# Four small moves in a fused recurrence and expert kernel: a store, six copies, two loads, and the first unit of the newer form

## The chip, the cores and the metric

The kernel runs on one core of one Trainium2 chip. The metric is the device time of one execution in microseconds; 962.84 us is the median of the three runs before the change.

## What is computed

A gated linear recurrence per batch and head feeds four dense experts whose outputs are mixed by normalised probabilities. Shapes: batch 4, 8 heads, 768 steps, head size 48; so x has 3072 rows of 384, and each expert goes 384 -> 1024 -> 384.

```python
for t in range(S):                       # per batch and head
    state = alpha[t][:, None] * state + outer(k[t], v[t])
    y[t] = q[t] @ state
x = y rearranged to (batch * step, head * 48)
p = domain_probs / (domain_probs.sum(-1) + 1e-9)
out = sum over e of p[:, e] * (relu(x @ w1[e]) @ w2[e])
```

## The kernel before, in words

**Units and groups.** The recurrence is cut into 24 units, each one block of 128 steps of one batch with all 8 heads (`units`, counted from 0). They are put into groups: group 0 has units 0 and 1, groups 1 to 5 have four units each (2 to 5, 6 to 9, and so on), group 6 the last two. The experts run over a group at a time (`tasks`): for each expert, `up` makes eight tiles of the hidden layer (L993, or L997 for the very first expert), and `down` multiplies them with w2 (L1081). In group 0 the first expert uses raw weights; after that every weight is split into two parts (ScalarE L261, VectorE L263) and stored for later groups by GpSimd (`kept<-w`, L264); later groups load the parts with SyncE (`w<-kept`, L234). In `up` from group 1 on, ScalarE makes the upper part of the hidden tile (L1001) and VectorE the lower one (L1033). VectorE's instruction is also the last reader of the PSUM tile `one`; `one` and the sums `ops` of `down` share four PSUM buffers, so the fifth tile of a row waits for the first L1033.

**The recurrence within a unit.** A unit's scores are built in seven levels of decay. Each level multiplies half of q and half of k by a factor (VectorE), makes the next level's factors (GpSimd, L788 or L557), copies q into block form (ScalarE, `qb`), and copies the half of the keys that stays the same. TensorE then makes score products, which VectorE takes under masks into `near`, and finally the unit's result and the update of the state.

There are two forms of a unit. `attention` (units 2 to 7 and, for the most part, 1) has four places on TensorE: scores of levels 0 to 3, then the last levels (L861 and L805), then a turn of the keys through TensorE (L295), then the result (L900, L481). `in_order` (from `in_fours`, unit 8, on) treats groups of four steps on GpSimd (L515, L518, L519; VectorE sums them in L529), so its levels 0 and 1 need no scores, and it turns the keys with VectorE (L639) and a round trip through DRAM: SyncE stores them as `over` (L648) and reads them back as `AT` (L655). All its TensorE work stands in one place, the step called the burst: the result of the unit before (L676, L695) and its own scores (L602, L612). Unit 0 is done by `first_unit` with an order of its own.

**What sets the order.** Each unit is a generator; `deal` gives each of its steps a planned time from a table of fractions, and `advance` runs the steps whose time has come while `up` and `down` are written out. Every engine executes its own instructions in the order written. For units 6 to 9 the ends are planned at 101.1, 132.8, 164.5 and 196.2, unit 5's at 63.4 and unit 4's at 50.7 (planned time, in which group 1's first expert begins at 69.4). An old-form unit begins at most two slots before its end; unit 6 begins at 50.7. A new-form unit has its burst at the end of the unit before and its head in the slot before that: the first one by `HEAD_FIRST` (first step at 0.06 of that slot), the second by `HEAD_SECOND`, all others by `HEAD_EARLY` and `HEAD`. `REST` places the steps after the burst in its own slot; the transpose L639 is at 0.17 of it, the store L648 at 0.3, the loads L655 at 0.58.

**Loads.** SyncE issues almost all loads, in order. Unit u's steps issue the loads of unit u + 1: an old-form unit alpha in its first step, k and q in its third; a new-form unit alpha in its second, k and q after the sums. For a new-form unit, q needs eight more transfers (L183, into two raw weight tiles that are then kept for it) and three of alpha (L186, into `row_a`, after GpSimd has set it to 1). An old-form unit from 6 on reads its q rows into the same memory (L175). Twelve raw weight tiles go round in `raws`; `whole_raw(keep=True)` takes one out for good.

**The start.** Unit 0 has no other work beside it on TensorE. Its `load_piece` calls carry `behind`: GpSimd copies one column of a computed tile into the raw tile (L241), so that the load of that piece begins only when the tile has been computed. Piece 0 waits for `QTs[4]`, pieces 1 to 3 for `later_half`. Then the first expert runs for unit 0 while unit 1's levels run on ScalarE, VectorE and GpSimd.

Of the kernel before, what the change touches and what calls it, by code (L numbers as in the profile page):

```python
# [10 lines left out]
F32 = mybir.dt.float32  # L11
# [9 lines left out]
def kernel(  # L21
# [11 lines left out]
    nc = tc.nc  # L33

    B, H, S, D = q.shape
    E, DM, F = moe_w1.shape
    P = 128
    NCB = S // P
    NP = H // 2
    HD = 64  # L40
    QUAD = 32
# [4 lines left out]
    NQ = 4  # L46
# [3 lines left out]
    HALF = P // 2  # L50
# [9 lines left out]
    t = np.arange(HALF)[None, :]  # L60
# [6 lines left out]
    dram = ctx.enter_context(tc.tile_pool(name="dram", bufs=1, space=bass.MemoryType.DRAM))  # L67
# [11 lines left out]
    xTs = {0: work.tile([P, 2, KC, NT], F32, name="xT", bufs=2)}  # L79
# [11 lines left out]
    half = B // 2  # L91
# [10 lines left out]
    NTOK = P // QUAD  # L102
# [38 lines left out]
    HEAD_SECOND = [0.02, 0.06, 0.1, 0.13, 0.16, 0.2, 0.25, 0.31, 0.37, 0.45, 0.52, 0.61, 0.66]  # L141
    REST = [0.05, 0.17, 0.3, 0.42, 0.58]
    in_runs = half + B
    in_fours = half + 2 * B - 2
    MARGIN = 6.0
    waiting = deque()
    clock = 0.0
# [47 lines left out]
    def expert(gi, e):  # L195
        return E - 1 - e if min(gi, LAST - 1) % 2 else e

    def stored(l, i):
        gi, k = divmod(i, E * NQ)
        e, c = divmod(k, NQ)  # L200
        return kept[l][expert(gi, e) * NQ + c]
# [7 lines left out]
    def whole_raw(keep=False):  # L209
        if keep:  # L210
            return raws.popleft()[1]
        raws.rotate(-1)
        return raws[-1][1]


    def parts_of(l):
        return wts.tile([P, 2, KC * QF], F32R, name=f"w{l + 1}", bufs=AHEAD if l == 0 else NQ)
# [4 lines left out]
    def load_piece(l, i, beside=False, held=None, behind=None):  # L222
        if i >= E * NQ * LAST:
            return
        gi, k = divmod(i, E * NQ)
        at, c = divmod(k, NQ)
        e = expert(gi, at)
        if at == 0 and gi > 0:
            if held is not None:
                wt[l][i] = held  # L230
            return
        if gi > l:
            w = wt[l][i] = parts_of(l)
            nc.sync.dma_start(out=w.bitcast(F32), in_=stored(l, i))  # L234
            return
        if l == 1 and gi == 0 and not beside:
            return
        w = whole_raw()
        wt[l][i] = w
        if behind is not None:  # L240
            nc.gpsimd.tensor_copy(out=w[:behind.shape[0], :1], in_=behind)  # L241
        if l == 0:
            nc.sync.dma_start(
                out=w.rearrange("p (c f) -> p c f", f=QF),
                in_=moe_w1[e].rearrange("(c p) f -> p c f", p=P)[:, :, c * QF:(c + 1) * QF])
        else:
            nc.sync.dma_start(
                out=w.rearrange("p (c d) -> p c d", d=DM),
                in_=moe_w2[e].rearrange("(c p) d -> p c d", p=P)[:, c * FPQ:(c + 1) * FPQ])
# [39 lines left out]
    def halves(t, m):  # L289
        return t.rearrange("p a (b two r) -> p a b two r", two=2, r=m)  # L290
# [7 lines left out]
    def first_unit(fill, other):  # L298
# [3 lines left out]
        for l in [0] * AHEAD + [1] * 2:  # L302
            t = parts_of(l).rearrange("p t x -> p (t x)")
# [7 lines left out]
        diag, later_half = (next(place_of).rearrange("p a (i n) -> p (a i) n", i=2) for _ in range(2))  # L311
# [29 lines left out]
        def next_k(li):  # L341
            old, new = (halves(t, LEVELS[li]) for t in (KTs[li], KTs[min(li + 1, 6)]))
            nc.vector.tensor_mul(new[:, :, :, 0, :], old[:, :, :, 0, :],
                                 spread(halved(decs[li])[:, :, :, 1], LEVELS[li]))
# [16 lines left out]
        def take(li, outs):  # L361
            for i in range(2):
                to = diag[:, NP * i:NP * (i + 1)]
                if li < 0:
                    nc.vector.copy_predicated(
                        to, masks_all[:, 6 * QUAD:].unsqueeze(1).broadcast_to([P, NP, HALF]), outs[i])
                    continue
                m = LEVELS[li]
                mk = masks[:, li, :].rearrange("p (b r) -> p b r", r=m)
                nc.vector.copy_predicated(  # L370
                    to.rearrange("p a (b two r) -> p a b two r", two=2, r=m)[:, :, :, 1, :],
                    mk.unsqueeze(1).broadcast_to([P, NP, QUAD // m, m]),
                    outs[i].rearrange("p a (b r) -> p a b r", r=m))
# [62 lines left out]
        products(5, part(third, QUAD))  # L436
        for i in range(2):
            nc.scalar.copy(out=later_half[:HALF, NP * i:NP * (i + 1)], in_=far[rows[i]])
        for i in range(1, NQ):
            load_piece(0, i, behind=later_half[:HALF, 0, :1])  # L440
        take(2, part(second, 0))
        take(3, part(second, QUAD))
        take(-1, part(second, HALF, HALF))
# [16 lines left out]
        for s, (past, scores) in enumerate(((keys[0], diag), (slice(0, P), later_half))):  # L460
            y = ps.tile([P, KC, HALF], F32, name=f"y{s}", tag="g", bufs=4)
            for n, turn in enumerate(zip(*terms)):
                for j, (c, h, at) in enumerate(turn):
                    nc.tensor.matmul(y[QUAD * j:QUAD * (j + 1), c], lhsT=flat_v[past, at:at + QUAD],
                                     rhs=scores[past, h], start=n == 0, stop=n == len(terms[0]) - 1)
            nc.scalar.copy(out=xTs[0][:, 0, :, HALF * s:HALF * (s + 1)], in_=y)
        next_k(6)
        return rest_of_first(AT, KTs[6], rv)

# [15 lines left out]
    def rest_of_first(AT, KT, rv):  # L485
        nc.scalar.copy(out=AT, in_=turned(lambda p: KT[:, p, :]))
        yield
        sps = key_values(AT, rv)
        for i in range(2):
            rows = slice(HD * i, HD * (i + 1))  # L490
            nc.vector.tensor_copy(out=sts[units[0][1]][rows, :, i, :], in_=sps[rows])
        load(2, "v")
        yield

    def in_order(u):
        cb, b = units[u]
        k = u - in_fours
        keep = cb < NCB - 1
# [61 lines left out]
        def next_k(li):  # L560
            m = LEVELS[li]
            old = new = halves(KTs[li], m)
            if 2 <= li < 6:
                KTs.append(work.tile([P, NP, P], F32, name="KT", bufs=6))
                new = halves(KTs[-1], m)
                nc.scalar.copy(out=new[:, :, :, 1, :], in_=old[:, :, :, 1, :])
            else:
                KTs.append(KTs[li])
            nc.vector.tensor_mul(new[:, :, :, 0, :], old[:, :, :, 0, :],
                                 spread(halved(decs[li])[:, :, :, 1], m))  # L570
# [63 lines left out]
        if keep:  # L634
            next_k(6)
            if not quads:
                quads.append(whole_raw(keep=True)[:, :NP * P])
            by_quad = quads[0].rearrange("x (t a c) -> x t a c", a=NP, c=QUAD)
            nc.vector.transpose(out=by_quad.rearrange("x t a c -> x a t c"),  # L639
                                in_=KTs[-1].rearrange("x a (t n) -> x a t n", n=QUAD))  # L640
        yield
        parts = lat.rearrange("p (r s i) c -> p r s i c", s=2, i=2)
        for s in range(2):
            rows = slice(HALF * s, HALF * (s + 1))
            nc.scalar.copy(out=parts[:HALF, :, s, :, HALF:], in_=far[rows])
        if keep:
            over = dram.tile([P, NTOK, NP * QUAD], F32, name="over", bufs=2)
            nc.sync.dma_start(out=over, in_=by_quad.rearrange("x t a c -> x t (a c)"))  # L648
        yield
        for s in range(2):  # L650
            rows = slice(HALF * s, HALF * (s + 1))
# [2 lines left out]
        for t in range(NTOK if keep else 0):  # L654
            nc.sync.dma_start(out=AT[QUAD * t:QUAD * (t + 1)],  # L655
                              in_=over.rearrange("(g r) t n -> t r g n", r=QUAD)[t])
# [60 lines left out]
    def attention(u):  # L717
# [28 lines left out]

        own = rk[:, :, :D]
        own_late = u == 1
        if not own_late:
            nc.gpsimd.tensor_mul(own, rq[:, :, :D], own)  # L750
        yield
# [39 lines left out]
        def next_k(li):  # L791
            m = LEVELS[li]
            old = new = halves(KTs[li], m)
            if li + 1 < len(LEVELS):
                KTs.append(keys())
                new = halves(KTs[-1], m)
                nc.scalar.copy(out=new[:, :, :, 1, :], in_=old[:, :, :, 1, :])
            nc.vector.tensor_mul(new[:, :, :, 0, :], old[:, :, :, 0, :],
                                 spread(halved(decs[li])[:, :, :, 1], m))

# [23 lines left out]
        for li in range(3):  # L824
            copy_q(li)
            next_q(li)
            next_k(li)
            yield
# [105 lines left out]
        if cb < NCB - 1:  # L934
            for i in range(2):
                rows = slice(HD * i, HD * (i + 1))
                old, add = st[rows, :, i, :], sps[rows]
# [189 lines left out]
    def deal():  # L1127
# [14 lines left out]
        for gis in [*([gi] for gi in range(1, LAST - 1)), [LAST - 1, LAST]]:  # L1142
# [6 lines left out]
            for k in range(n):  # L1149
# [4 lines left out]
                if u >= in_fours:  # L1154
# [9 lines left out]
                    events += [(time, u, run) for time in times[-1]]  # L1164
                    continue
                run = attention(u)
                beats = [0.0, *BEATS]
                due_at = {-1: begin, **{j: begin + (end - begin) * beats[j + 1] for j in (7, 11, 16)}}
# [20 lines left out]
    with tc.manual_schedule():  # L1189
# [21 lines left out]
        def fill(times, n=P):  # L1211
            for _ in range(times):
                nc.tensor.matmul(idle[:, :n], lhsT=zeros[:, :P], rhs=zeros[:, :n], start=True, stop=True)

        runs = [None, attention(1)]
        fill(7)
        runs[0] = first_unit(fill, runs[1])

        span = cost(0, 0, 0) * FCH / 2 + cost(1, 0, 0)
# [51 lines left out]
```

## Time and profile before

| | |
|---|---|
| runs before, median (lowest to highest) | 962.84 us (962.35 to 963.54) |
| the profiled execution: its time, its span | 963.35 us, 961.6 us |
| TensorE granted clock | 1.00 |

Busy time by stage, from the profile's stretches (us):

| stage | length | PE | DVE | ACT | POOL |
|---|---|---|---|---|---|
| 0 to 18.9: unit 0 | 18.90 | 16.38 | 12.03 | 9.66 | 7.35 |
| 18.9 to 45.75: first expert, unit 0's rows, and on | 26.85 | 25.68 | 15.22 | 19.46 | 6.49 |
| 45.75 to 138.1: the rest of group 0 | 92.35 | 90.94 | 65.23 | 69.56 | 27.20 |
| 138.1 to 287.8: group 1 | 149.70 | 146.53 | 104.97 | 71.73 | 61.13 |
| 287.8 to the end | 673.80 | 669.17 | 326.42 | 207.88 | 171.87 |

How to read it: PE is TensorE, DVE VectorE, ACT ScalarE, POOL GpSimd, SP SyncE; a q behind an engine's name is its queue of issues. Busy time counts modelled ends of matrix products. A row of the timeline gives the start, the duration, the engine, the line, the operation, what it writes and reads, the shape and how many instructions were merged; in square brackets stands the idle time ahead of it and what ended that. A row of the waits gives who waited for whom, the total in us, the number of times, and the longest.

### The profile page before, as it was taken

What the parts mean: (1) busy time and instruction counts of PE and PEld (TensorE: products, weight loads), DVE (VectorE), ACT (ScalarE), POOL (GpSimd) and SP (SyncE); (2) the same over time, 40 slices, a digit from 0 to 9 for tenths busy, and PEclk for the clock granted to TensorE, in tenths of its full rate; (3) what the DMA queues carried; (4) which work ended last, traced back from release to release, by engine and by line L of the source; (5) the groups of instructions that cost most, each with busy time, mean ns of one, the idle gap of its engine ahead of it and who ended that gap; (6) DMA issues with size and microseconds to landing.
All of it is one profiled execution on the core that took longest, in us unless ns stands there. A gap on an engine that the chain in (4) does not pass through costs nothing.

```text
span 961.6 us, 21086 instructions
## 1 busy us (share of the span) xinstructions
PE 948.7 (99%) x8456; PEld 854.5 (89%) x8456; DVE 523.9 (54%) x971; ACT 378.3 (39%) x825; POOL 274.0 (28%) x379
## 2 busy tenths in 40 slices
PE   8999999999899999999999999999999999999998
PEld 7788778898888989989989889899899899999997
DVE  5667767577656655655646646647674312221222
ACT  5787756445154253242441441444244212121111
POOL 3232332443443441532523414415441000000000
PEclk9999999999999999999999999999999999999999
DMA  7899758798876687755786864678970007070701
GB/s 172 265 336 289 234 149 257 233 339 235 278 230 188 182 303 223 230 177 149 214 280 190 289 209 119 197 238 222 283 229 18 26 2 261 1 263 1 261 19 33
DMA packets 172037, 188.09 MB, mean 196 GB/s; under 512 B 83436, under 2 KB 151404, under 8 KB 171940
## 3 DMA queue, kind: packets, MB, share of 16 engines
q1 hardware_dynamic: 165476, 156.89, 54.1%
q0 software_dynamic: 6016, 29.49, 8.1%
q8 instruction: 67, 1.10, 0.5%
q10 hardware_dynamic: 448, 0.36, 0.1%
q14 instruction: 30, 0.25, 0.1%
HBM read 153.67 MB, written 33.03 MB: 194 GB/s over the span
## 4 chain that ended last, share of the span: by engine, by line
PE 88%; DMA 4%; DVE 3%; ACT 2%; issue 1%; SPq 0%; POOL 0%; DVEq 0%; ACTq 0%; POOLq 0%
PE ops L1081 39%; PE one L993 38%; PE sc L602 3%; PE yps L676 3%; PE sc L805 2%; DMA raw<-in_moe_w_dram 1%; DMA kept<-w 1%; PE tp L295 1%; DMA over<-raw 1%; ACT qb L779 1%; PE yps L900 1%; DMA AT<-over 1%; PE sps L612 1%; DMA sq<-in_q_dram 0%; PE sps L695 0%
## 5 line engine op out<-in xcount | busy, mean ns | idle before, releaser
L1081 PE MATMUL ops<-w,hT 128*128 128x384 f32 x2112 | 375.8, 337 | 0.6 <-DVE hT L1033 0.6
L1081 PEld LDWEIGHTS ops<-w,hT 128*128 128x128 f32 x2112 | 365.6, 188 | 5.3 <-issue 2.4
L993 PE MATMUL one<-xT,w 128*128 128x512 f32 (+1 forms) x1656 | 361.4, 377 | 0.0
L993 PEld LDWEIGHTS one<-xT,w 128*128 128x128 f32 x1656 | 296.4, 188 | 57.1 <-issue 0.3
L1001 ACT ACTIVATE hT<-one 128x512 fp32r<-128x512 f32 (+3 forms) x232 | 120.8, 524 | 319.7 <-PE one L993 317.8
L1033 DVE SCALAR_TENSOR_TENSOR hT<-one,hT 128x512 fp32r<-128x512 f32 (+1 forms) x192 | 120.4, 641 | 105.8 <-ACT hT L1001 105.7
L557 POOL TENSOR_TENSOR AT<-AT 128x256 f32<-128x256 f32 (+2 forms) x66 | 30.8, 467 | 199.1 <-DVE QT L555 199.0
L1107 DVE SCALAR_TENSOR_TENSOR acc<-ops,p_all,acc 128x384 f32<-128x384 f32 x66 | 38.8, 611 | 77.0 <-PE ops L1081 76.9
L555 DVE TENSOR_TENSOR QT<-QT,AT 128x256 f32<-128x256 f32 x77 | 37.5, 487 | 69.0 <-ACT qb L549 50.8
L1116 POOL DMA_DIRECT2D out_dram<-acc x22 | 12.0, 550 | 205.3 <-DVE acc L1107 205.3
L519 POOL TENSOR_TENSOR raw<-raw,rk 128x768 f32<-128x768 f32 x32 | 60.2, 1882 | 2.5
L518 POOL TENSOR_TENSOR raw<-raw,ra 128x576 f32<-128x576 f32 x32 | 50.9, 1592 | 1.3
L779 ACT COPY qb<-QT 64x256 f32<-64x256 f32 x98 | 40.1, 410 | 14.9 <-DVE QT L786 11.8
L1081 PE MATMUL ops<-raw,hT 128*128 128x384 f32 x128 | 45.6, 494 | 0.0
L549 ACT COPY qb<-QT 64x256 f32<-64x256 f32 x88 | 35.3, 401 | 16.2 <-DVE QT L555 12.5
L557 POOL TENSOR_TENSOR raw<-raw 128x256 f32<-128x256 f32 (+5 forms) x30 | 14.0, 466 | 97.1 <-DVE raw L555 97.1
L529 DVE TENSOR_REDUCE dot<-raw 128x16 f32<-128x768 f32 x32 | 29.7, 931 | 19.8 <-POOL raw L519 19.8
L264 POOL DMA_DIRECT2D kept<-w x32 | 18.7, 585 | 68.4 <-DVE w L263 33.1
L788 POOL TENSOR_TENSOR AT<-AT 128x256 f32<-128x256 f32 (+5 forms) x42 | 19.5, 464 | 60.6 <-DVE QT L786 60.4
L685 ACT CAST xT<-yps 128x384 fp32r<-128x384 f32 x14 | 6.7, 479 | 74.5 <-PE yps L676 74.5
L993 PE MATMUL one<-raw,w 128*128 128x256 f32 x288 | 35.2, 283 | 0.0
L993 PEld LDWEIGHTS one<-raw,w 128*128 128x128 f32 x288 | 35.1, 192 | 0.0
(168 smaller groups left out, 975.6 us busy)
## 6 DMA issues: line engine op xcount, KB each, us to landing
w<-kept SPq DMA_DIRECT2D x108, 768.0 KB, 6.8
kept<-w POOLq DMA_DIRECT2D x32, 768.0 KB, 5.7
raw<-in_moe_w_dram SPq DMA_DIRECT2D x44, 384.0 KB, 7.0
raw<-in_q_dram SPq DMA_DIRECT2D x128, 96.0 KB, 2.9
rv<-in_v_dram SPq DMA_DIRECT2D x24, 192.0 KB, 3.5
out_dram<-acc POOLq DMA_DIRECT2D x22, 192.0 KB, 2.5
rk<-in_k_dram SPq DMA_DIRECT2D x18, 192.0 KB, 3.2
sa<-in_alpha_dram SPq DMA_DIRECT2D x36, 88.0 KB, 3.2
```

Of the source, the lines that this page charges most:

```text
L518: nc.gpsimd.tensor_mul(t[:, :, 1:], t[:, :, 1:], row_a[:, some])
L519: nc.gpsimd.tensor_mul(t, t, row_k[:, some].unsqueeze(2).broadcast_to([P, H // 2, FOUR, D]))
L529: nc.vector.reduce_sum(out=dots[:, some], in_=t, axis=AX.X)
L549: nc.scalar.copy(out=qbs[li][rows, :, i, :].rearrange("p a (b r) -> p a b r", r=m), in_=qv[rows])
L555: nc.vector.tensor_mul(qv, qv, spread(dv[:, :, :, 0], m))
L557: nc.gpsimd.tensor_mul(dec, dv[:, :, :, 0], dv[:, :, :, 1])
L779: nc.scalar.copy(out=qb[rows, :, i, :].rearrange("p a (b r) -> p a b r", r=m), in_=qv[rows])
L993: nc.tensor.matmul(one, lhsT=w[:, of_w, kc], rhs=x_part(gi, of_x)[:, kc, :n], start=k == 0, stop=k == len(turns) - 1)
L1001: nc.scalar.activation(out=parts[0], in_=one, func=ACT.Relu)
L1033: nc.vector.scalar_tensor_tensor(out=low, in0=x, scalar=0.0, in1=top.bitcast(F32), op0=ALU.max, op1=ALU.subtract)
L1081: nc.tensor.matmul(sums[slot], lhsT=h, rhs=w, start=(n == begins[slot]), stop=(n == ends[slot]))
L1107: nc.vector.scalar_tensor_tensor(out=acc, in0=part, scalar=scale, in1=acc, op0=ALU.mult, op1=ALU.add)
```

## The change

Four edits. The planned time of the newer form begins one unit earlier: `in_fours` goes from 8 to 7. In the start, raw pieces 2 and 3 of the first expert wait for the first half of unit 0's x in place of `later_half`. The store of the turned keys goes from SyncE to GpSimd's queue, and from the step of the `lat` copies to the step before, right behind the transpose. In unit 1, GpSimd copies the unchanged half of the keys in six levels in place of ScalarE.

```diff
-    in_fours = half + 2 * B - 2
+    in_fours = half + 2 * B - 3
...
-        for i in range(1, NQ):
-            load_piece(0, i, behind=later_half[:HALF, 0, :1])
+        load_piece(0, 1, behind=later_half[:HALF, 0, :1])
...
             nc.scalar.copy(out=xTs[0][:, 0, :, HALF * s:HALF * (s + 1)], in_=y)
+            if s == 0:
+                for i in range(2, NQ):
+                    load_piece(0, i, behind=xTs[0][:, 0, 0, :1])
...
                                 in_=KTs[-1].rearrange("x a (t n) -> x a t n", n=QUAD))
+            over = dram.tile([P, NTOK, NP * QUAD], F32, name="over", bufs=2)
+            nc.gpsimd.dma_start(out=over, in_=by_quad.rearrange("x t a c -> x t (a c)"))
...
-        if keep:
-            over = dram.tile([P, NTOK, NP * QUAD], F32, name="over", bufs=2)
-            nc.sync.dma_start(out=over, in_=by_quad.rearrange("x t a c -> x t (a c)"))
...
+        copy_k = nc.gpsimd.tensor_copy if u == 1 else nc.scalar.copy
...
-                nc.scalar.copy(out=new[:, :, :, 1, :], in_=old[:, :, :, 1, :])
+                copy_k(out=new[:, :, :, 1, :], in_=old[:, :, :, 1, :])
```

## The prediction

> **What bounds the kernel now.** First the page's busy line and its 40 slices, then the waits of TensorE. Units are counted from 0, as in the code: the second is unit 1, the eighth unit 7.
>
> ```profile
> PE 948.7 (99%) x8456; PEld 854.5 (89%) x8456; DVE 523.9 (54%) x971; ACT 378.3 (39%) x825; POOL 274.0 (28%) x379
> ...
> PE   8999999999899999999999999999999999999998
> ```
>
> TensorE has work in 948.7 of 961.6 us, and the clock row shows 9 in every slice. Only two things can shorten such a kernel: less work on TensorE, or the removal of its few waits. After the first 18.9 us the waits that matter are these:
>
> ```profile
> PE sps L695 <- DMA AT<-over: 2.5, 1, 2.5
> ...
> PE far L861 <- ACT qb L779: 1.0, 1, 1.0
> PE ops L1081 <- DVE hT L1033: 0.6, 1, 0.6
> ```
>
> They stand at 251 us (unit 8), 30 us (unit 1) and 199 us. By stage the busy times leave TensorE 1.2 us idle from 18.9 to 45.75 us and 3.2 us in group 1 (138.1 to 287.8). So whatever the other engines gain, about 4 us of waits is all there is to win, beside TensorE's own work.
>
> **GpSimd stores the moved keys, one step earlier.** The 2.5 us is a chain on SyncE's queue (timeline of SP):
>
> ```profile
> 227.37 6.62 SPq L183 DMA_DIRECT2D raw<-in_q_dram  x8
> 234.03 3.09 SPq L186 DMA_DIRECT2D ra<-in_alpha_dram  x3
> 237.22 0.55 SPq L234 DMA_DIRECT2D w<-kept  x1
> 237.87 1.16 SPq L648 DMA_DIRECT2D over<-raw  x1
> 239.12 1.55 SPq L234 DMA_DIRECT2D w<-kept  x2
> 245.96 1.97 SPq L655 DMA_DIRECT2D AT<-over  x4
> ```
>
> The keys were transposed by VectorE at 227.05 to 227.76, but the store L648 stood behind the next unit's loads until 237.87. It took 8.0 us to land, L655 waited for it to 245.96, and its last piece landed 6.0 us after 247.44; TensorE had been ready at 251.0. On GpSimd, idle there until a multiply at 228.21, the store goes at about 227.8. GpSimd's own stores (kept<-w, three times the bytes) land in 5.7 us in the median, these on SyncE in 8.1: landing is at 234 to 236. L655 then goes when SyncE is free, at 240.7, and lands 7.5 us later as now, at 248.2, 2.8 us before it is needed. Gain 2.5 us. In the new plan this place belongs to unit 7, one slot earlier, with the same queues. GpSimd pays 13 issues of 0.59 us (the kept<-w row) in an engine 28% busy; each waits for a VectorE transpose, and what is queued behind it on GpSimd (that multiply, for VectorE at 229.8) waits for a later VectorE instruction anyway. At nothing; if the cover failed, 0.6 us a unit.
>
> **The newer form from unit 7 on.** In the old form TensorE does unit 7 in four places, from which these are the second and third:
>
> ```profile
> 192.16 0.66 PE L861 MATMUL far<-qb,KT 128*64 128x128 f32 x8
> 192.65 1.10 PE L805 MATMUL sc<-qb,KT 128*64 128x64 f32 x32
> ...
> 204.00 0.60 PE L295 MATMUL tp<-ident,KT 128*128 128x128 f32 x4
> ```
>
> By the chain of waits the first (scores, 169.97 to 171.99) lasts 2.02 us, these 1.52 and 0.44, the last (the result, 209.04 to 211.04) 2.00: 5.98 us. The new form does all in one place, 4.46 us in steady state (yps at 288.23 to the next L1081 at 292.69). Gain 1.5 us, sure. The wait at 199 us arose while the first new-form unit's head ran beside old-form unit 7; in that slot there is now a second new-form head, as at 225 to 245, which has no such wait: gain 0.6.
>
> The cost comes one slot earlier. A new-form unit begins with six products on GpSimd (two L515, then L518 and L519 twice; the first and the last row):
>
> ```profile
> 176.92 2.11 POOL L515 TENSOR_TENSOR ra<-ra 128x384 f32<-128x384 f32 x2
> ...
> 183.93 1.92 POOL L519 TENSOR_TENSOR raw<-raw,rk 128x768 f32<-128x768 f32 x1
> ```
>
> This block of 8.9 us waits for L186's loads. Unit 8's were issued by 168.1, long before 176.9. Unit 7's own head is planned much closer to its loads: by the code's formula its first step is at 101.1 - 0.94 x 37.7 = 65.7 of planned time, and its loads are at unit 6's third step, 59.0. On the trace that step's loads are here:
>
> ```profile
> 127.86 2.00 SPq L170 DMA_DIRECT2D sq<-in_q_dram  x4
> 129.90 1.84 SPq L175 DMA_DIRECT2D ra<-in_q_dram  x1
> ```
>
> In place of L175 come eight L183 and three L186 from 129.9 on. Issued at their medians (0.60 and 0.61, with gaps of 0.05) they take 7.2 us, and as in the three bursts seen (6.75 + 1.92 and more) 8.7 to 9.9. The last L186 lands 2.8 us after its start (median; 2.3 to 5.4). So the block starts at 139.3 to 140.9; its extremes are 138.2 and 144.8. I take 140.1. GpSimd would otherwise be ready at about 134.
>
> Behind it on VectorE's queue are the two reductions (5.5 and 8.9 us into the block), and behind the block on GpSimd the factor that unit 6's next multiply needs. Between them stand the L1033 of group 1's first matrix stage, which free the four PSUM buffers. The second one now ends at 145.4; it would end at 140.1 + 8.9 + 0.9 (reduction) + 0.7 (two multiplies) + 0.9 (two takes) + 0.7 = 152.2. TensorE wants that buffer for the sixth of its eight tiles at 144.2 + 3 x 2.05 = 150.35: 1.8 us late. The third comes 3.8 us after (turn of q 0.95, multiply 0.6, two more 0.7, takes 0.9, itself 0.7), at 156.0, when TensorE wants it at 152.2 + 2.05 = 154.2: 1.7 late. The fourth is then in time. **Cost 3.5 us**, with 1.7 at 138.2 and 8.2 at 144.8.
>
> **GpSimd copies unit 1's keys.** ScalarE drops six copies of 0.41 us between 21.0 and 30.0. No GpSimd copy of 128x256 is in the trace; below is its one-column copy (0.18 us), above the 128x256 product (0.72 us in this unit). I take 0.47, the usual product. A level's chain is two qb copies and a VectorE multiply, about 1.3 us, where the first levels now take 1.4 us; but TensorE's own work stands between until 27.3, and the last levels hang on VectorE's takes:
>
> ```profile
> 28.91 0.89 DVE L815 COPY_PREDICATED near<-masks,sc 128x256 f32<-128x256 uint8 x2
> 29.70 0.42 DVE L786 TENSOR_TENSOR QT<-QT,AT 128x256 f32<-128x256 f32 x1
> ```
>
> So of the 1.0 us before L861 only part can go: gain 0.6, between 1.2 (all of that stage's idle) and a loss of 2.2: VectorE products beside GpSimd work are at times long (2.08 us at 184.06, beside L519, where the line's mean is 0.45), and six copies of 0.47 could hold VectorE for 2.8 us in all. The Trainium skill (SBUF — State Buffer, Who interferes with whom) says that a VectorE operation with two SBUF inputs and a GpSimd operation that reads SBUF contend for one pair of ports, and that the one that comes second is blocked until the first is done. By that rule the term could be the loss of 2.2 and the sum +1.1; the product at 184.06 agrees with it, and no row here shows a GpSimd copy of this size beside VectorE.
>
> **Two raw pieces wait for x.** They are issued at 16.13 and 17.04 now, after it from about 17.9 (the ACT copy of y ends at 17.66, a GpSimd copy 0.2, SyncE free). The fifth and seventh tile need them at about 21.8 and 23.5. Alone the first piece landed 3.1 us after issue, so 21.0 and, one piece (1.5 us at 260 GB/s) later, 22.5 to 23.5. Nothing, between 0.5 gained (a wait of 0.27 us marked "issue" while five pieces are in flight) and 1.0 lost.
>
> **Sum.** -2.5 - 1.5 - 0.6 - 0.6 + 3.5 = -1.7 us, from the profiled 963.35 (span 961.6 and 1.75 around it) to 961.6. The median of the runs, 962.84, is 0.5 lower: forecast **961.1 us**. A measurement of this kernel tells 0.2% (1.9 us) from no change, so this is just within it; half a microsecond of the block's start decides.
>
> **Rivals.**
> - *The loads come in time* (24%): the block starts near 138, or VectorE's slack takes it. Cost 0 to 1.5, sum -5.2 to -3.7: 957.6 to 959.1. For it: few transfers run from 130 to 138 us. Against: eleven issues on one queue take at least 6.6 us.
> - *Slower* (14%): the block starts at 144.8, if L186 takes its longest landing, 5.4 us. Then 8.2 of stall, +3.0: 965.8. The sign turns at a start of 141.8, and 0.2% is passed at about 143.7. For it: the issue of 1.84 us in that queue, and 5.4 us once seen.
> - *The store's wait doesn't go* (5%), so the change doesn't do what it says: L655 is still late, since L247's pieces share the transfers. Then +0.8: 963.6. Against: 2.8 us to spare.
> - *GpSimd's copies hold VectorE* (5%), by 2.8 us in unit 1: +1.1, 963.9. For it the row at 184.06; against, ScalarE's 2.5 us of relief in the same stage.
> - *The forecast* (52%): 960 to 962.5, two thirds of it within 0.2%.
>
> Faster: 24 and a third of 52, 41%; same: two thirds of 52 and the two of 5, 45%; slower 14%. Range 957.6 to 965.0, which leaves out little but the slower rival.
>
> **What would show it.** Right: no wait at L695; the L861 and L805 of unit 7 gone (L805 672 to 576, L602 1024 to 1088); the first L515 at about 140, VectorE waiting for L519 there, and TensorE waiting in L993 for L1033 near 150 to 155. Wrong: L515 before 138 or after 143, or TensorE waiting in the first 50 us for raw pieces.

## The result, and the profile after

The changed kernel takes **967.13 us** (median of 6 runs, 965.83 to 969.60), the kernel before 962.08 beside it (6 runs): a ratio of 1.005, 95% interval 1.0036 to 1.0064. It is slower, by 5 us (0.5%) where 1.7 us of gain were forecast, and outside the range. Its profiled execution took 967.25 us (span 965.5), 3.9 more than the one of before (963.35), and the account below is of these two. Lines behind the start's code have moved by up to four: L1035, L995 and L1083 are L1033, L993 and L1081 of before, L517 and L521 are L515 and L519, L656 is L655.

The page's busy line and TensorE's 40 slices of the kernel after:

```profile
PE 949.2 (98%) x8420; PEld 853.7 (88%) x8420; DVE 523.5 (54%) x971; ACT 373.4 (39%) x812; POOL 291.9 (30%) x403
...
PE   8999998999999999999999999999999999999998
```

TensorE has 36 products fewer, yet is as long busy, and one slice in group 1 (the seventh, 145 to 169 us) is no longer full. Its waits from 18.9 us on:

```profile
PE one L995 <- DVE hT L1035: 3.1, 3, 2.6
PE sps L696 <- DMA AT<-over: 2.1, 2, 1.3
...
PE sps L614 <- issue: 1.2, 1, 1.2
PE far L863 <- ACT qb L781: 1.1, 1, 1.1
```

Two of them were not there before: the waits of `one`, the tiles of `up`, for VectorE's L1035 (before, only `ops` waited for that instruction, once, for 0.6 us), and a wait in L614 for nothing that the profile shows ("issue"). The wait for AT, which was to go, now comes twice, each time smaller (1.28 us at unit 7, 0.79 at unit 8).

**The first hidden stage of group 1.** GpSimd's products for unit 7 and the loads before them (timelines of GpSimd and of SyncE):

```profile
139.65 2.85 POOL L517 TENSOR_TENSOR ra<-ra 128x384 f32<-128x384 f32 x2 [5.38 <-DMA ra<-in_alpha_dram]
...
147.39 1.84 POOL L521 TENSOR_TENSOR raw<-raw,rk 128x768 f32<-128x768 f32 x1
```

```profile
129.60 6.26 SPq L183 DMA_DIRECT2D raw<-in_q_dram  x8
135.96 1.92 SPq L186 DMA_DIRECT2D ra<-in_alpha_dram  x3
```

GpSimd stood idle for 5.38 us until alpha's loads landed. The block started at 139.65, where 140.1 was forecast, and ended at 149.2. Behind it, VectorE and TensorE (their timelines; idle time ahead of a row in brackets):

```profile
149.27 0.95 DVE L531 TENSOR_REDUCE dot<-raw 128x16 f32<-128x768 f32 x1 [1.76 <-POOL raw L521]
...
152.09 0.71 DVE L1035 SCALAR_TENSOR_TENSOR hT<-one,hT 128x512 fp32r<-128x512 f32 x1
```

```profile
152.85 3.51 PE L995 MATMUL one<-xT,w 128*128 128x512 f32 x9 [2.55 <-DVE hT L1035]
```

The second L1035 ended at 152.8 (forecast: 152.2), and TensorE had waited 2.55 us for its PSUM buffer. Then came what no step of the prediction had. This is the stretch of time behind it: its length, the busy time and number of instructions of PE, PEld, DVE, ACT and POOL, then the granted clock, DMA share and GB/s.

```profile
153.00:157.00 4.00, 3.70 (x10) 2.46 (x11) 3.93 (x8) 1.81 (x5) 0.36 (x1) 0.59 1.02 413
```

Behind the idle time the clock was granted at 0.59 on average: half of it for 3.4 us, from 153.71 us on.

**The store and its loads.** SyncE's queue for unit 8, as shown of before:

```profile
227.12 5.15 SPq L183 DMA_DIRECT2D raw<-in_q_dram  x8
232.31 1.94 SPq L186 DMA_DIRECT2D ra<-in_alpha_dram  x3
...
234.99 7.09 SPq L234 DMA_DIRECT2D w<-kept  x4
242.25 1.99 SPq L656 DMA_DIRECT2D AT<-over  x4
```

The store went out on GpSimd at 232.37 and had landed by 235.28, in 2.9 us (forecast: 6 to 8). The loads L656 went at 242.25, but the three whose landing the profile shows landed only at 255.1 to 255.7, 12.5 to 12.9 us after their own issue; of before, the last one landed 6.0 us after its issue.

The change of length by stage, from the starts of the expert's stages on TensorE:

| stage | before | after | |
|---|---|---|---|
| to group 1's first hidden stage | 137.66 | 137.36 | -0.30 |
| that stage | 20.52 | 25.35 | +4.83 |
| from there to group 1's last `up` | 103.13 | 101.17 | -1.96 |
| the rest, to the end of the execution | 702.04 | 703.37 | +1.33 |

### The profile page after: what moved, and what is told of

Same layout as the page of the kernel before. It is cut to its first block, busy times and chain, and to the rows that moved or that the text cites. A ratio compares the mean times of both kernels' runs of the same rounds, so it can differ in the third digit from the quotient of the medians.

```text
span 965.5 us, 21056 instructions
## 1 busy us (share of the span) xinstructions
PE 949.2 (98%) x8420; PEld 853.7 (88%) x8420; DVE 523.5 (54%) x971; ACT 373.4 (39%) x812; POOL 291.9 (30%) x403
## 4 chain that ended last, share of the span: by engine, by line
PE 87%; DMA 4%; ACT 3%; DVE 2%; issue 2%; SPq 1%; POOL 1%; DVEq 0%; POOLq 0%; ACTq 0%
PE ops L1083 38%; PE one L995 37%; PE sc L604 4%; PE yps L677 3%; DMA AT<-over 2%; PE sc L807 1%; DMA raw<-in_moe_w_dram 1%; PE tp L295 1%; SPq L183 1%; PE sps L614 1%; PE one L999 1%; PE yps L902 1%; ACT qb L781 1%; PE sps L696 1%; ACT hT L1003 0%
## 5 line engine op out<-in xcount | busy, mean ns | idle before, releaser
L1083 PE MATMUL ops<-w,hT 128*128 128x384 f32 x2112 | 375.2, 337 | 0.2
L1083 PEld LDWEIGHTS ops<-w,hT 128*128 128x128 f32 x2112 | 365.6, 188 | 5.1 <-issue 3.1
L995 PE MATMUL one<-xT,w 128*128 128x512 f32 (+1 forms) x1656 | 363.5, 378 | 3.1 <-DVE hT L1035 3.1
L995 PEld LDWEIGHTS one<-xT,w 128*128 128x128 f32 x1656 | 297.2, 189 | 61.8 <-DVE hT L1035 4.6
L1035 DVE SCALAR_TENSOR_TENSOR hT<-one,hT 128x512 fp32r<-128x512 f32 (+1 forms) x192 | 120.1, 640 | 108.4 <-ACT hT L1003 108.3
L559 POOL TENSOR_TENSOR AT<-AT 128x256 f32<-128x256 f32 (+2 forms) x72 | 33.4, 463 | 193.3 <-DVE QT L557 189.1
L557 DVE TENSOR_TENSOR QT<-QT,AT 128x256 f32<-128x256 f32 x84 | 39.8, 474 | 76.4 <-ACT qb L551 46.3
L521 POOL TENSOR_TENSOR raw<-raw,rk 128x768 f32<-128x768 f32 x34 | 63.9, 1879 | 2.7
L520 POOL TENSOR_TENSOR raw<-raw,ra 128x576 f32<-128x576 f32 x34 | 53.7, 1580 | 1.3
L531 DVE TENSOR_REDUCE dot<-raw 128x16 f32<-128x768 f32 x34 | 31.7, 934 | 31.4 <-POOL raw L521 31.4
L551 ACT COPY qb<-QT 64x256 f32<-64x256 f32 x96 | 38.6, 402 | 18.4 <-DVE QT L557 14.7
L1083 PE MATMUL ops<-raw,hT 128*128 128x384 f32 x128 | 45.5, 493 | 0.0
L781 ACT COPY qb<-QT 64x256 f32<-64x256 f32 x84 | 34.4, 410 | 20.0 <-DVE QT L788 16.3
L517 POOL TENSOR_TENSOR ra<-ra 128x384 f32<-128x384 f32 x34 | 36.1, 1062 | 6.8 <-DMA ra<-in_alpha_dram 5.4
L995 PE MATMUL one<-raw,w 128*128 128x256 f32 x288 | 35.2, 283 | 0.0
L995 PEld LDWEIGHTS one<-raw,w 128*128 128x128 f32 x288 | 35.1, 192 | 0.0
(173 smaller groups left out, 965.5 us busy)
```

Source lines behind the costliest of these rows:

```text
L520: nc.gpsimd.tensor_mul(t[:, :, 1:], t[:, :, 1:], row_a[:, some])
L521: nc.gpsimd.tensor_mul(t, t, row_k[:, some].unsqueeze(2).broadcast_to([P, H // 2, FOUR, D]))
L551: nc.scalar.copy(out=qbs[li][rows, :, i, :].rearrange("p a (b r) -> p a b r", r=m), in_=qv[rows])
L557: nc.vector.tensor_mul(qv, qv, spread(dv[:, :, :, 0], m))
L559: nc.gpsimd.tensor_mul(dec, dv[:, :, :, 0], dv[:, :, :, 1])
L781: nc.scalar.copy(out=qb[rows, :, i, :].rearrange("p a (b r) -> p a b r", r=m), in_=qv[rows])
```

## The experiments

Theory 1 after the result: the loss is the stall in group 1's first hidden stage, made by GpSimd's block that waits for alpha's loads, with the half clock behind it; the other edits cost nothing. Theory 2: the store on GpSimd's queue and SyncE's freed queue crowd the transfers. Theory 3: the start's edits cost. Each kernel was run beside the kernel before, and each ratio below is to that; the times are medians of 6 to 12 runs, with the kernel before at 962.26 to 962.66 in these three sessions.

**Unit 7 in the older form**, the three other edits kept:

```diff
-    in_fours = half + 2 * B - 3
+    in_fours = half + 2 * B - 2
```

> The changed kernel with unit 7 back in the older form (in_fours 8): the store, the six copies and the two raw pieces stay as changed. Theory 1 (the loss is the stall in group 1's first hidden stage, where GpSimd's block for unit 7 waits for alpha's loads, with the half clock behind it; the other edits cost nothing): 960.8 to 961.8 us, no granted clock below full in 140 to 165 us, and the products of unit 8 wait for the loads of AT at most as long as before (2.5 us). Theory 2 (the store on GpSimd's queue and SyncE's freed queue crowd the transfers, and that is the loss): about 965 us, with waits for AT as in the changed kernel. Theory 3 (GpSimd's copies or the later raw pieces cost the start): over 963.5 us, with the loss already there at 45.7 us.

961.3 us, ratio 0.9987 (0.9975 to 1.0). The stage at 138 us has its old length (+0.00), and the waits of TensorE from 137 to 275 us are:

```profile
PE sps L696 <- DMA AT<-over: 1.5, 1, 1.5
PE ops L1083 <- DVE hT L1035: 0.6, 1, 0.6
```

So the loss comes with the newer form of unit 7; the moved store, the copies and the raw pieces lose nothing that the runs can tell. Theories 2 and 3 fall.

**The newer form alone**, in the kernel before:

```diff
-    in_fours = half + 2 * B - 2
+    in_fours = half + 2 * B - 3
```

> The kernel before with the newer form from unit 7 on (in_fours 7) and nothing else. Theory 1 (the stall behind alpha's loads, with the half clock): 965 to 968 us: stall 3.5 + clock 1.3 - 1.5 for the fewer places on TensorE, and waits for AT of 1 to 2.5 us at unit 7 as at unit 8; TensorE waits about 2.5 us for VectorE's L1033 near 153 us. Theory 2 (the loss is the crowding by the moved store): about 960 to 961 us, without a wait for AT over 2.5 us in all. Theory 3 (the start): as theory 2.

969.72 us, ratio 1.0067 (1.0046 to 1.0088): more than the 965 to 968 us expected. The profiled execution (967.35 us) is one of two with a mean clock of 0.999 or more; the other four had 0.995 to 0.998 and took 969.0 to 973.0 us. The wait in the stage at 138 us, and the stretch behind the first part of it:

```profile
PE one L993 <- DVE hT L1033: 3.7, 2, 2.3
```

```profile
153.00:157.00 4.00, 2.34 (x9) 1.61 (x9) 3.93 (x8) 1.90 (x5) 0.36 (x1) 1.00 0.98 370
```

Here the clock stayed at 1.00, and yet the stage is 4.42 us longer than before: from the start of one product to the start of the next, less the usual distance, the two places cost 2.44 and 1.61 us, where the forecast had 1.8 and 1.7; the rest is products behind the waits that follow each other a little more slowly. In the changed kernel the half clock cost the stage only 0.4 more, since a slower TensorE came late for the third buffer anyway (0.3 us of wait there).

**The store alone**, in the kernel before, in the step of the transpose:

```diff
+            over = dram.tile([P, NTOK, NP * QUAD], F32, name="over", bufs=2)
+            nc.gpsimd.dma_start(out=over, in_=by_quad.rearrange("x t a c -> x t (a c)"))
...
-        if keep:
-            over = dram.tile([P, NTOK, NP * QUAD], F32, name="over", bufs=2)
-            nc.sync.dma_start(out=over, in_=by_quad.rearrange("x t a c -> x t (a c)"))
```

> The kernel before with the store of the turned keys on GpSimd's queue, one step earlier, and nothing else. Theory 1 (the store costs nothing; the loads of AT come late because other loads share the transfers, so that little of the 2.5 us wait is won): 961 to 962.3 us, the wait of unit 8's products for AT between 0.5 and 2 us. Theory 2 (the store or SyncE's freed queue crowds the transfers): 964 us or more. The prediction's own term (the wait goes): 959.6 to 960.2 us, no wait for AT.

962.3 us, ratio 0.9992 (0.9981 to 1.0003). The loads of AT (L655 of before) went at 239.61 in place of 245.96, but landed at 250.9 and later in place of 253.4: 6.3 us earlier out, some 2 earlier in. The wait was 0.7 us in this profile, 1.9 less than in the profile of before, and yet the gain of 2.5 is not there in the medians.

**Alpha's loads ahead of q's**, in the changed kernel (the loop L186 moved above the loop L183):

```diff
+            for j in range(FOUR - 1):
+                nc.sync.dma_start(out=row_a[j::FOUR].rearrange("p h f d -> p h (f d)")[:, :, D * j:],
+                                  in_=by_four(alpha)[:, :, D * (j + 1):])
             for i, t in enumerate(fours[u]):
...
-            for j in range(FOUR - 1):
-                nc.sync.dma_start(out=row_a[j::FOUR].rearrange("p h f d -> p h (f d)")[:, :, D * j:],
-                                  in_=by_four(alpha)[:, :, D * (j + 1):])
```

> The changed kernel with the three loads of alpha for a newer-form unit issued ahead of the eight of q instead of behind them. Theory 1: GpSimd's block for unit 7 starts about 134 to 136 us rather than 139.7, VectorE's second reduction is done by about 145 rather than 149.3, TensorE's wait for L1033 near 153 us falls from 2.55 to under 0.5 us and the half clock goes: 962 to 963.5 us (the waits for AT stay). If the half clock comes without the wait, about 964. Theory 2 (crowding by the moved store): 966 to 967 us, since the same bytes move.

963.81 us, ratio 1.0009 (0.9997 to 1.0022), so 3.3 us below the changed kernel, which ran in a session of its own, and a little above the 962 to 963.5 expected. The block no longer waits for alpha, but the wait for L1035 fell only to 1.4 us. GpSimd's and VectorE's timelines:

```profile
134.10 2.14 POOL L517 TENSOR_TENSOR ra<-ra 128x384 f32<-128x384 f32 x2
...
142.09 2.43 POOL L521 TENSOR_TENSOR raw<-raw,rk 128x768 f32<-128x768 f32 x1
```

```profile
138.27 4.56 DVE L263 TENSOR_TENSOR w<-raw,w 128x768 fp32r<-128x768 f32 x2
142.75 2.32 DVE L833 TENSOR_TENSOR near<-ident,dot 128x512 f32<-128x512 f32 x1
```

The block ends 4.7 us earlier, the second reduction on VectorE only 2.6 (147.6 for 150.2): VectorE's three products took 6.9 us beside the block, where the changed kernel's took 3.3 (1.82 for the two of L263, begun at 138.4 with GpSimd idle until 139.65, and 1.51 for L833 beside L517; in the kernel before, with no product of GpSimd beside it, that one took 0.69). The Trainium skill (SBUF — State Buffer, Who interferes with whom) states that a VectorE operation with two SBUF inputs and a GpSimd operation that reads SBUF share a pair of ports and block each other; these rows agree.

**The two raw pieces and the six copies alone**, in the kernel before:

```diff
-        for i in range(1, NQ):
-            load_piece(0, i, behind=later_half[:HALF, 0, :1])
+        load_piece(0, 1, behind=later_half[:HALF, 0, :1])
...
+            if s == 0:
+                for i in range(2, NQ):
+                    load_piece(0, i, behind=xTs[0][:, 0, 0, :1])
...
+        copy_k = nc.gpsimd.tensor_copy if u == 1 else nc.scalar.copy
```

> The kernel before with the two raw pieces behind x and the six copies on GpSimd, and nothing else. The prediction's term: 0.6 us faster (961.7 against 962.3). Theory 1, from the changed kernel's stages (0.3 us gained by 137 us): 961.8 to 962.3 us, the wait of L861 for qb still about 1 us since VectorE's takes hold that chain. Rival of the prediction (GpSimd's copies hold VectorE): 963 to 964.5 us with VectorE's products in 21 to 31 us longer than 0.6 us.

962.35 us against 962.62, ratio 0.9995 (0.998 to 1.0011). By 137 us the profile has gained 0.63, and the wait of `far` for qb is still 1.0: no gain that the runs can tell, and no loss. One copy came while a VectorE product was running (rows of both timelines):

```profile
24.15 0.92 DVE L834 TENSOR_TENSOR near<-ident,dot 128x512 f32<-128x512 f32 x1
24.46 0.86 POOL L800 COPY KT<-KT 128x256 f32<-128x256 f32 x1
```

The other five copies took 0.39 to 0.42 us: here it is the copy, which came second, that waited. In this kernel SyncE stores as before, yet unit 8's wait was 1.1 us, not 2.5 (the profile names GpSimd's L521, long done; AT's loads landed at 251.4, when it ended), so the size of that wait seems to differ from one execution to the next.

**The loads of AT earlier**, in the kernel with unit 7 in the older form:

```diff
-    REST = [0.05, 0.17, 0.3, 0.42, 0.58]
+    REST = [0.05, 0.17, 0.3, 0.42, 0.42]
```

> The changed kernel with unit 7 in the older form (961.3 us in its own run) and the loads of AT planned at 0.42 of the slot rather than 0.58, so that SyncE issues them ahead of two of the three weight loads of 768 KB that stood before them. Theory 1 (the loads of AT come late because they stand behind those weight loads in the shared transfers: 13 us from issue to landing where 0.25 MB alone would need about 6): the AT loads land before 250 us, the wait of unit 8's products for them (1.5 us in the profile) goes, 959.5 to 960.2 us. Rival (the transfers are full there, whatever comes first; the delayed weight loads are then late): 961 us or more, with a new wait of TensorE for a w piece or for raw pieces at 250 to 262 us.

960.75 us against 961.3, ratio to before 0.9977 (0.9964 to 0.9991). SyncE's queue, and all waits of TensorE from 137 to 275 us:

```profile
236.74 0.55 SPq L234 DMA_DIRECT2D w<-kept  x1
237.45 3.23 SPq L656 DMA_DIRECT2D AT<-over  x4
240.78 0.85 SPq L234 DMA_DIRECT2D w<-kept  x2
```

```profile
PE ops L1083 <- DVE hT L1035: 0.6, 1, 0.6
```

With one weight load of 768 KB ahead of them rather than three, the loads (64 KB each) landed in 5.9 to 6.9 us, at 244.4 to 245.1 (three of the four show), and the wait is gone; behind it only one product of the burst (L604, at 253 us) came 0.3 us later than before. The gain in the median is smaller than expected (0.6 for 1.1 to 1.8), and between two sessions 0.6 us is no more than the runs can tell. The Trainium skill (DMA: Bandwidth & Descriptors, Queues, rings and completion order) states that on each DMA engine the descriptors of one issuing row are consumed in ring order; the loads behind the weights agree.

**The head later**, in the changed kernel:

```diff
-    HEAD_FIRST = [*(0.06 * j for j in range(1, 8)), 0.5, 0.58, 0.66, 0.74, 0.82, 0.93]
+    HEAD_FIRST = [0.40, 0.43, 0.56, 0.62, 0.64, 0.66, 0.69, 0.73, 0.78, 0.84, 0.89, 0.94, 0.98]
```

> The changed kernel with the first head of the newer form planned later in its slot (its first step at 0.40 rather than 0.06, the last at 0.98), so that GpSimd's block for unit 7 comes behind the factors that unit 6's levels need. Theory 1 (the stall in group 1's first hidden stage is made by that block, in front of unit 6's factors on GpSimd and of L1035 on VectorE): no wait of TensorE for L1035 at 150 to 157 us, 961 to 962.5 us (967.1 - 4.5 - up to 1 for the half clock), unless unit 7's burst is late instead, which would show as a wait of TensorE for qb or KT at its scores. Theory 2 (crowding by the moved store): 966 to 967 us.

967.37 us, ratio 1.0048 (1.0029 to 1.0068): a miss. The stall at 150 us is gone, and another of 3.0 us stands at 191 us, in the next hidden stage. Rows of GpSimd and VectorE there, and the stretch with the end of the wait:

```profile
180.51 2.11 POOL L517 TENSOR_TENSOR ra<-ra 128x384 f32<-128x384 f32 x2 [2.84 <-DMA ra<-in_alpha_dram]
```

```profile
186.09 0.95 DVE L531 TENSOR_REDUCE dot<-raw 128x16 f32<-128x768 f32 x1 [4.13 <-POOL raw L521]
...
193.95 0.65 DVE L1035 SCALAR_TENSOR_TENSOR hT<-one,hT 128x512 fp32r<-128x512 f32 x1
```

```profile
194.00:198.00 4.00, 3.35 (x10) 2.65 (x11) 4.00 (x8) 0.00 (x0) 1.76 (x3) 0.70 0.76 255
```

It is the same chain one unit on: the steps of unit 7's head also issue unit 8's loads, so now unit 8's block waits for alpha, with L531 ahead of L1035. The mechanism is confirmed, the cure is not: later does not help, since the loads move too. The wait before L614 at 664 us was 2.1 us in this profile.

**The head later and the loads of AT earlier**, in the changed kernel:

```diff
+    HEAD_FIRST = [0.40, 0.43, 0.56, 0.62, 0.64, 0.66, 0.69, 0.73, 0.78, 0.84, 0.89, 0.94, 0.98]
...
+    REST = [0.05, 0.17, 0.3, 0.42, 0.42]
```

> The later head and the earlier loads of AT together, all four edits of the change kept. If both causes are what theory 1 says: 959.5 to 961 us, with no wait for L1035 at 150 us and under 0.5 us for AT at 218 and 255 us; what would be left against the best is the wait of 0.5 to 1.5 us marked issue at 660 us. If only the stall was the cause: as the later head alone, 961 to 962.5 us.

965.73 us, ratio 1.0025 (1.0011 to 1.0038). The waits for AT are gone (none from 200 to 262 us), the one for L1035 at 191 us is 3.1, and the clock was halved for 6.8 us from 193.8 on. A miss in its time (959.5 to 961 expected), since the stall stays.

**32 products more at the start**: in the changed kernel, unit 0's first score products are issued twice, so that all later ones stand 32 further on in TensorE's stream.

```diff
-        products(0, part(first, 0))
+        for _ in range(2):
+            products(0, part(first, 0))
```

> The changed kernel with the 32 score products of unit 0's first level issued twice (same inputs and output), in the start, so that every later instruction of TensorE has a place 32 further on in its stream. In every profile with the newer form from unit 7 on, TensorE waited 0.3 to 2.1 us, marked issue, in unit 20's burst behind product 6410 or 6411 of its stream; in none of the others. Theory 1 (that wait hangs on the place in the stream, which the change moves by 36 products): it is gone from that burst, and from 160 us on the kernel is 1.2 to 1.4 us shorter than the changed one; 966 us with the 0.3 us or so that the products themselves cost. Rival (it hangs on the work of that burst): the wait of about 1.2 us stays before the same L614, 967.1 to 967.5 us.

967.17 us, ratio 1.005 (1.0033 to 1.0068). The wait before L614 at 664 us is gone, but a new one has come at 258.7 us, in unit 8's burst (L605 is L604 of the changed kernel):

```profile
PE sc L605 <- issue: 0.7, 1, 0.7
```

So these waits move with the place in the stream and do not hang on the work alone: with the newer form from unit 7 on they stand behind product 6407 to 6411 in each of six profiles; with the added products behind 2872, here and in a later run, and behind 2872 also in the two kernels of the older plan whose AT comes early (0.3 and 1.1 us). The page counts 66 transfers of its queue for instructions, 16 KB each, and one of these began at 662.85 us in the changed kernel and had ended at 664.26, 0.4 us before TensorE stopped. Whether TensorE waits for such blocks of instructions is not shown; the cause stays open. The total gained nothing (966 us expected), as the rival had it: one place was exchanged for another.

**Alpha first, another order, and the loads of AT earlier**: all four edits of the change, with the alpha loop first, `REST` as above, and

```diff
+    HEAD_FIRST = [0.06, 0.12, 0.24, 0.30, 0.36, 0.39, 0.42, 0.5, 0.58, 0.66, 0.74, 0.82, 0.93]
```

> All four edits, with alpha's loads ahead of q's, the first newer-form head's two reductions and its turn of q planned 2 us later or so (so that L1035 comes ahead of each on VectorE), and the loads of AT at 0.42. Theory 1 (the rest of the stall with alpha first, 1.4 us, is VectorE's row of reductions, levels and turn ahead of the third L1035; the waits for AT are the weight loads ahead of them): TensorE's wait for L1035 under 0.4 us at 150 to 157 us, under 0.3 us for AT; 960 to 961.5 us with the wait marked issue at 660 us still there. Rival (GpSimd's block beside VectorE makes VectorE's own rows long, so the stall stays whatever the order): a wait of 1 us or more for L1035, 962 us or more.

960.29 us, ratio 0.9975 (0.996 to 0.999): the lowest median here, 6.8 us below the changed one; the next two, 960.51 and 960.75, are too close to tell apart. All its waits from 137 us on:

```profile
PE one L995 <- DVE hT L1035: 0.5, 2, 0.3
PE sps L614 <- issue: 0.4, 1, 0.4
PE ops L1083 <- DVE hT L1035: 0.2, 1, 0.2
```

L1035 now comes ahead of each reduction; the first three start at 143.31, 147.49 and 150.43, which is 3.5, 4.6 and 5.5 us earlier than in the changed kernel, although VectorE's three products still took 5.3 us beside the block (6.9 with alpha first, 3.3 in the changed kernel). The rival falls.

**The same with the 32 products**:

```diff
-        products(0, part(first, 0))
+        for _ in range(2):
+            products(0, part(first, 0))
```

> As the run with all four edits, alpha first, the later reductions and the earlier loads of AT, with unit 0's 32 products twice. If the wait marked issue hangs on the place in the stream: it is gone, and the time is 0.3 to 1 us below that run, 959.3 to 960.8 us. If not: the same to 0.4 us above it.

961.57 us, ratio 0.9984 (0.9973 to 0.9996), 1.3 slower than without: the wait marked issue left 657 us (0.4) and stands at 253 (0.8), the start is 1.2 longer, and one wait for L1035 grew from 0.3 to 0.9. A miss: the wait marked issue moved and did not go.

**Alpha first in the kernel with unit 7 in the older form and early loads of AT**:

```diff
-    in_fours = half + 2 * B - 3
+    in_fours = half + 2 * B - 2
...
-    REST = [0.05, 0.17, 0.3, 0.42, 0.58]
+    REST = [0.05, 0.17, 0.3, 0.42, 0.42]
```

and the alpha loop moved as above.

> The newer form from unit 8 on (as before), the store, copies and raw pieces as changed, the loads of AT at 0.42, and alpha's loads ahead of q's. Against the same without alpha first (960.75 us): 0.3 to 0.8 us shorter, 960.0 to 960.4, if the last wait for L1035, 0.6 us at 199 us, stands behind GpSimd's block as the stall of the changed kernel does; no difference if it hangs on something else.

960.51 us, ratio 0.998 (0.997 to 0.9991), 0.2 below the same without alpha first, less than the runs can tell. The wait of 0.6 us for L1035 at 198 us stays, so it does not hang on alpha. This profile also has two waits marked issue, of 1.1 us at 252 us and 0.4 at 440, so a small gain elsewhere could be hidden in the total.

## Why the prediction was wrong

By its own steps, in the two profiled executions:

- **The store and L655: forecast -2.5, measured -0.2.** This is the step that failed most: "L655 then goes when SyncE is free, at 240.7, and lands 7.5 us later as now". With the store alone it went at 239.61, as forecast, and landed at 250.9 and later, not at 248.2. In the changed kernel unit 7's loads, where the step put the gain, went from 205.02 to 207.28 us, and the one whose landing shows took 12.2 us; unit 8's took up to 12.9. In before the loads went out when the first of the three weight loads ahead of them had landed (245.2 us; the second landed at 248.7); sent earlier, they stand behind three or four of 768 KB that have not, and the earlier load kept little of its lead. From start to start of the products around it the place lost 2.81 us before, and 1.54 and 1.06 at units 7 and 8 now. Early AT alone, with L234 behind rather than in front, took the wait away. The rival that had this at 5% named L247's pieces, which are issued after L656; it was L234 ahead of it. Besides, the 2.5 us was one execution's: it was 1.1 in the profile of another kernel with the same store.
- **The block: forecast +3.5, measured +4.8 with the half clock, 4.4 without (the newer form alone).** Mechanism, place and both buffers are as the step had them; the start was 0.45 us early, the block 0.7 longer than the 8.9 us taken, and VectorE's chain behind it 0.4 longer. Without this cost the change would have gained 0.8 us; with the forecast 3.5 it would still have lost 2.7. The half clock was in no step.
- **The wait at 199 us: forecast -0.6, measured +0.2.** It came back in three pieces (0.37, 0.32 and 0.26, from start to start, for 0.78).
- **The older form's places on TensorE: forecast -1.5, measured about -1.9** (the stretch's -1.96 less the two terms above); L805's successor has 576 products, L604 has 1088, as said.
- **Copies and raw pieces: forecast -0.6 and 0, measured -0.3.** This is within what the profiles differ by: with the same start, unit 7 in the older form reached that stage 0.3 us later than before. Neither TensorE nor VectorE waits for them; `far` still waits 1.1 us.
- **Not in the sum: +1.4** at 664 us (1.45 from start to start), the wait marked issue. It came in every profile with the newer form of unit 7 and no added products; why TensorE waits there stays open.

The sum of these is +4.0 for the +3.9 between the two profiled executions. Of the 5.6 us between -1.7 and +3.9, the store's step is 2.3, the wait marked issue 1.4, the stall 1.3, the wait at 199 us 0.8; the other two, -0.4 and +0.3, nearly cancel. The slower rival had 14% and hung on one thing, a later start of the block; the start came as forecast. What it left out is that the sign turns just as well when the two gains of 2.5 and 0.6 fail, without the block moving at all. And those gains were in reach: with alpha first, the reductions behind L1035 and AT ahead of most of the weights, the same four edits are faster than before, by 0.25%.

## What to carry to other kernels

A load sent earlier is not one that lands earlier: look at what its own queue has issued just before, in bytes, and put a small load that is needed soon ahead of the large ones. When a block of work on one engine waits for a load, follow every queue behind it, and order the short instruction that frees a buffer ahead of the one that waits. A wait seen in one execution is at most a bound on the gain, not the gain.

## What the runs showed of the hardware that was not expected

- **The clock after a short wait.** An idle time of TensorE of 2.55 us was followed by half the clock for 3.41 us, which began 0.86 us after the idle time had ended. With the later head, idle times of 3.0 and 2.1 us were each followed by 3.41 us of it; with the later head and AT earlier, 6.8 us of it began within the last 0.7 us of an idle time of 3.1. Idle times of 2.3 us (the newer form alone, and 32 products more) and the 2.55 us of before were not followed by any. Over all executions, a mean clock of 0.998 or less was granted in 28 of 54 executions of the kernels whose profile has a wait of 1.6 us or more (the changed one, the newer form alone, alpha first, both with the later head, 32 products more), and in 7 of 83 of the others. The kernel before, with 2.5 us in its profile, had it in 28 of 94. In the last session it had it in 9 of 30, and took 964.8 us there (median) for 962.2 in the other 21. So such a wait seems to cost more in the mean than its own length; that it sets the clock off is read from the order of events in three profiles, and was not tried by itself. The Trainium skill (TensorE: Matmul & The Clock Gate, What's actually happening) gives an idle window of about 3.4 us as what halves the clock; here 2.55 us did in one execution and not in another.
- **Places in TensorE's stream** at which it waits 0.3 to 2.1 us with nothing to wait for, within bursts of short products: the same place, within four products, in each kernel with the same count ahead of it. What it waits for is not shown.
